# One PSUM tile for each unit's outputs, 64-row stores, and a last block emptied by VectorE and stored on two queues

## The chip, the cores and the metric

The kernel runs on one core of one Trainium2 chip. The metric is the device time of one execution in microseconds, less is better. A result is the median of several executions; all of those told here were fast ones. Every result was correct against the reference.

Engine names in the profile: PE is TensorE (PEld its weight loads), DVE is VectorE, ACT is ScalarE, POOL is GpSimd, SP is SyncE; a q behind the name is the engine's sequencer, which also issues DMAs.

## The reference, cut to what matters

An RWKV-5 attention (batch 4, 8 heads, 768 steps, head size 48) is followed by a dense block on 3072 rows of 384:

```python
x = attn_out.transpose(0, 2, 1, 3).reshape(3072, 384)
h = x @ w_in                 # 384 x 2048
g = h - np.tanh(h)
out = g @ w_out              # 2048 x 384
```

This text is about the last product and how its results leave the chip.

## The kernel before

The kernel works in 24 *units* of 128 rows, two units to a *block* (12 blocks). Every unit holds 64 steps of two batches, so its 128 output rows are two runs of 64 rows in memory. The dense part of a block goes in *tiles* of two slices of 128 of the 2048 columns: h (12 TensorE records), then five ScalarE and four VectorE steps that make g, then o (8 records). In the trace one fp32 matmul of the program shows as two records (768 records of o for 384 matmuls).

The first six blocks are done in four passes, a quarter of the columns each, because the weights are still being converted; their partial sums are kept in SBUF and VectorE adds each pass (`part`). So outputs are emptied 60 times from PSUM: 12 times by ScalarE and 36 times by VectorE in the passes, 12 times by ScalarE for the last six blocks.

```python
def o(self, t, half):
    if t.first and half == 0:
        pair = self.ps_d.tile([128, L, 512], F32, name="o", tag="o", bufs=1)   # both units
        self.outs = [pair[:, i, : self.d.DM] for i in range(L)]
    # the last tile finishes unit 0 (half 0) before unit 1 (half 1)
    for z, i in [(0, half), (1, half)] if t.last else [(half, 0), (half, 1)]:
        self.nc.tensor.matmul(self.outs[i], t.g2[:, z, i * C : (i + 1) * C], ...)

def empty(self, t, i):
    ...                                                  # VectorE adds in passes 2 to 4
    self.nc.scalar.copy(t.o, self.outs[i])

def store(self, t, i, queue):
    runs = self.rows(L * t.j + i)                        # two runs of 64 rows
    n, step = C // len(runs), runs[-1] - runs[0] or C
    to = bass.AP(tensor=self.out.tensor, offset=...,
                 ap=[[step * self.d.DM, len(runs)], [self.d.DM, n], [1, self.d.DM]])
    queue.dma_start(out=to, in_=t.o)                     # GpSimd; SyncE in the last block
```

`pair` holds 512 fp32 columns of PSUM for each unit. The framework that places the waits treats it as one tile: a write to it waits for earlier reads of it, whichever unit they were for.

In which order the instructions stand on each engine is decided on the host while the program is built. A small planner plays the list of tasks through with assumed costs and improves the order in 600 random tries with a fixed seed (`Random(3)`). The planner knows nothing of PSUM tiles. A change in the list of tasks therefore gives another order everywhere; a change in how a task is carried out does not.

At the end, every engine loads a flag and branches: a general path follows that is not taken here.

## Time and profile before

| of the kernel before | |
|---|---|
| time, median | 641.43 us (4 runs, 640.81 to 641.90) |
| span in the profile | 638.85 us |
| TensorE busy | 600.5 us, 94% |
| VectorE, ScalarE busy | 67%, 63% |
| last matmul ends | 625.18 us, 13.67 us before the end |

TensorE is the bound, so I read everything by what stops TensorE and by what follows its last matmul. The lines themselves are in the prediction. Two lines of the list of DMA issues are worth adding (out<-in, engine, count, size, median us from issue to landing): the stores of 192 KB on GpSimd's queue took over 7 us, while loads of half the size landed in 3.

```profile
rt<-in_r_dram SPq DMA_DIRECT2D x48, 96.0 KB, 3.1
...
out_dram<-part POOLq DMA_DIRECT2D x12, 192.0 KB, 7.5
out_dram<-o POOLq DMA_DIRECT2D x10, 192.0 KB, 7.7
```

### The profile page before, as it was taken

What the parts mean: (1) busy time and instruction counts of PE and PEld (TensorE: products, weight loads), DVE (VectorE), ACT (ScalarE), POOL (GpSimd) and SP (SyncE); (2) the same over time, 40 slices, a digit from 0 to 9 for tenths busy, and PEclk for the clock granted to TensorE, in tenths of its full rate; (3) what the DMA queues carried; (4) which work ended last, traced back from release to release, by engine and by line L of the source; (5) the groups of instructions that cost most, each with busy time, mean ns of one, the idle gap of its engine ahead of it and who ended that gap; (6) DMA issues with size and microseconds to landing.
All of it is one profiled execution on the core that took longest, in us unless ns stands there. A gap on an engine that the chain in (4) does not pass through costs nothing.

```text
span 638.9 us, 13183 instructions
## 1 busy us (share of the span) xinstructions
PE 600.5 (94%) x5297; PEld 442.1 (69%) x5297; DVE 430.1 (67%) x698; ACT 401.0 (63%) x875; POOL 56.1 (9%) x115
## 2 busy tenths in 40 slices
PE   8779999999999999999999999999999999999991
PEld 7657776676666666766777767777777777777760
DVE  5799887989895878665767665566755564645550
ACT  3487778868645656455764765666774667565550
POOL 3001111200000000001022011002010001011000
PEclk9999999999999999999999999999999999999996
DMA  7974796623310000001331220112210100000000
GB/s 128 177 163 94 133 189 119 131 59 103 99 50 0 1 1 1 1 2 38 68 75 35 58 44 8 44 33 39 51 32 1 33 8 9 24 7 8 20 0 30
DMA packets 92498, 33.76 MB, mean 53 GB/s; under 512 B 84900, under 2 KB 86384, under 8 KB 92428
## 3 DMA queue, kind: packets, MB, share of 16 engines
q1 hardware_dynamic: 82208, 27.34, 21.9%
q0 software_dynamic: 10208, 5.49, 3.6%
q8 instruction: 43, 0.70, 0.5%
q14 instruction: 27, 0.22, 0.1%
q10 hardware_dynamic: 12, 0.00, 0.0%
HBM read 26.94 MB, written 4.72 MB: 50 GB/s over the span
## 4 chain that ended last, share of the span: by engine, by line
PE 77%; DVE 10%; ACT 7%; issue 3%; DMA 1%; POOL 0%; DVEq 0%; ACTq 0%; POOLq 0%
PE o L202 33%; PE h L164 33%; PE yk_ps L564 5%; PE x_ps L606 3%; PE x_ps L564 1%; ACT tg L177 1%; DVE g L188 1%; DVE tg L190 1%; ACT s L173 1%; PE h L505 1%; ACT th L175 1%; DVE part L210 1%; DVE tg L192 1%; DVE g L194 1%; DVE rT L610 1%
## 5 line engine op out<-in xcount | busy, mean ns | idle before, releaser
L202 PE MATMUL o<-w_out_sb,g 128*128 128x384 f32 x768 | 283.3, 493 | 9.9 <-DVE part L210 8.5
L164 PE MATMUL h<-xt,w_in_sb 128*128 128x256 f32 x1152 | 281.3, 381 | 2.0 <-DVE w_in_sb L139 2.0
L164 PEld LDWEIGHTS h<-xt,w_in_sb 128*128 128x128 f32 x1152 | 216.2, 190 | 64.3 <-issue 2.2
L202 PEld LDWEIGHTS o<-w_out_sb,g 128*128 128x128 f32 x768 | 141.8, 191 | 79.3 <-DVE part L210 14.6
L188 DVE TENSOR_TENSOR g<-h,th 128x512 f32<-128x512 f32 x96 | 66.0, 687 | 78.6 <-ACT s L173 59.1
L177 ACT ACTIVATE tg<-h 128x512 f32<-128x512 f32 x96 | 57.0, 594 | 77.2 <-PE h L164 77.1
L190 DVE SCALAR_TENSOR_TENSOR tg<-s,tg 128x512 f32<-128x512 f32 x96 | 65.9, 686 | 47.6 <-ACT tg L177 25.1
L173 ACT ACTIVATE s<-h 128x512 f32<-128x512 f32 x96 | 57.3, 597 | 48.7 <-PE h L164 48.6
L175 ACT ACTIVATE th<-h 128x512 f32<-128x512 f32 x96 | 57.2, 595 | 31.1 <-PE h L164 30.9
L194 DVE COPY_PREDICATED g<-small,tg 128x512 f32<-128x512 int32 x96 | 70.4, 733 | 6.0 <-DVE tg L192 0.5
L192 DVE SCALAR_TENSOR_TENSOR tg<-q,tg 128x512 f32<-128x512 f32 x96 | 66.0, 688 | 7.5 <-ACT q L179 3.6
L179 ACT ACTIVATE q<-s,m1b 128x512 f32<-128x512 f32 x96 | 69.6, 725 | 0.7
L181 ACT ACTIVATE small<-s,smallb 128x512 f32<-128x512 f32 x96 | 69.4, 723 | 0.3
L706 POOL DMA_DIRECT2D xt<-rest x66 | 32.9, 505 | 223.8 <-ACT rest L692 223.8
L630 ACT ACTIVATE at<-same,du 128x64 f32<-128x64 f32 x160 | 41.8, 342 | 3.1 <-DVE du L626 2.8
L223 POOL DMA_DIRECT2D out_dram<-part x12 | 9.7, 808 | 218.6 <-DVE part L210 218.6
L610 DVE TENSOR_TENSOR rT<-x_ps,w_up 128x512 f32<-128x512 f32 x23 | 15.8, 686 | 12.7 <-PE x_ps L606 9.9
L210 DVE TENSOR_TENSOR part<-o,part 128x384 f32<-128x384 f32 x36 | 19.9, 552 | 6.0 <-PE o L202 6.0
L564 PEld LDWEIGHTS yk_ps<-at,vt 64*64 64x64 f32 x752 | 13.2, 134 | 12.7 <-DVE at L741 5.2
L564 PEld LDWEIGHTS yk_ps<-rT,state 48*64 48x64 f32 x704 | 12.3, 134 | 12.2 <-DVE state L712 5.6
L618 ACT COPY kT<-x_ps 128x512 f32<-128x512 f32 x22 | 12.9, 588 | 12.3 <-PE x_ps L606 7.6
L690 ACT COPY xt<-yk_ps 128x192 f32<-128x192 f32 x22 | 7.0, 320 | 21.1 <-PE yk_ps L564 20.9
(104 smaller groups left out, 427.5 us busy)
## 6 DMA issues: line engine op xcount, KB each, us to landing
st<-in_moe_w_out_dram SPq DMA_DIRECT2D x8, 768.0 KB, 7.0
rt<-in_r_dram SPq DMA_DIRECT2D x48, 96.0 KB, 3.1
vt<-in_v_dram SPq DMA_DIRECT2D x48, 96.0 KB, 3.2
st<-in_moe_w_in_dram SPq DMA_DIRECT2D x16, 288.0 KB, 5.5
kt<-in_k_dram SPq DMA_DIRECT2D x44, 96.0 KB, 3.5
out_dram<-part POOLq DMA_DIRECT2D x12, 192.0 KB, 7.5
out_dram<-o POOLq DMA_DIRECT2D x10, 192.0 KB, 7.7
st<-in_moe_w_in_dram SPq DMA_DIRECT2D x16, 96.0 KB, 5.4
```

The source lines that it names most:

```text
L164: self.nc.tensor.matmul(t.h2[:, z], self.w_in_sb[:, t.f // 2, kk, z * 128 : (z + 1) * 128], self.xts[t.j][:, kk].rearrange("p b t -> p (b ...
L173: A.activation(out, t.h, AF.Square)
L175: A.activation(out, t.h, AF.Tanh)
L177: A.activation(out, t.h, AF.Tanh, scale=G1)
L179: A.activation(out, t.s, AF.Square, bias=self.m1b)
L181: A.activation(out, t.s, AF.Relu, bias=self.smallb, scale=-1.0)
L188: V.tensor_tensor(t.g, t.h, t.th, ALU.subtract)
L190: V.scalar_tensor_tensor(t.tg, t.s, C4, t.tg, ALU.mult, ALU.mult)
L192: V.scalar_tensor_tensor(t.tg, t.q, K1, t.tg, ALU.add, ALU.mult)
L194: V.copy_predicated(t.g, t.small.bitcast(I32), t.tg)
L202: self.nc.tensor.matmul(self.outs[i], t.g2[:, z, i * C : (i + 1) * C], self.w_out_sb[:, t.f + z, :], start=t.first and z == 0, stop=t.last ...
L564: T.matmul(*args, skip_group_check=True, **how)
```

## The change

Its intent: unit 0 may be emptied while unit 1 is still being written; a store may use more of the DMA engines; and the last block, after which nothing else comes, may leave by the shortest way.

```diff
     def o(self, t, half):
         if t.first and half == 0:
-            pair = self.ps_d.tile([128, L, 512], F32, name="o", tag="o", bufs=1)
-            self.outs = [pair[:, i, : self.d.DM] for i in range(L)]
+            self.outs = [self.ps_o().tile([128, 512], F32, name=f"o{i}", tag=f"o{i}", bufs=1)[:, : self.d.DM]
+                         for i in range(L)]
...
-        self.nc.scalar.copy(t.o, self.outs[i])
+        if t.j == self.d.NB - 1:
+            self.nc.vector.tensor_copy(t.o, self.outs[i])
+        else:
+            self.nc.scalar.copy(t.o, self.outs[i])
-    def store(self, t, i, queue):
...            (one transfer of two runs)
+    def store(self, o, n, z, queue):
+        runs = self.rows(n)
+        size = C // len(runs)
+        queue.dma_start(out=self.out[runs[z] : runs[z] + size, :], in_=o[z * size : (z + 1) * size])
...
-                by = "SP" if j == d.NB - 1 else "POOL"
-                stored[j, i] = [add(by, .6, send, [x.empty[-1]], due + 4 * pace, data=.8)]
+                by = ["SP", "ACT"] if j == d.NB - 1 else ["POOL"] * 2
+                stored[j, i] = [add(by[z], .6, ..., [x.empty[-1]], due + 4 * pace, data=.4) for z in range(2)]
```

(Cut: a tile of 2 x 512 columns serves the first attention units before, from a pool of its own that is closed at the first output. The planner's task for the last emptying moves to VectorE. One `pace` is rewritten to the same value, and a call in the path that is not taken changes its arguments.) Since the tasks change, the search finds another order.

More of the change, by code (lines that the diff above doesn't have):

```diff
@@ L142, with __init__ @@
 class Dense:
-    def __init__(self, nc, work, gpool, ps_d, shared, out, rows):
-        self.nc, self.work, self.gpool, self.ps_d = nc, work, gpool, ps_d
+    def __init__(self, nc, work, gpool, ps_d, shared, out, rows, ps_o=None):
+        self.nc, self.work, self.gpool, self.ps_d, self.ps_o = nc, work, gpool, ps_d, ps_o or (lambda: ps_d)
         self.out, self.rows, self.xts, self.sums = out, rows, {}, {}
@@ L215, in empty @@
             t.o = self.sums[at] = self.work.tile([128, self.d.DM], F32, name="part", tag="part", bufs=L * FIRST)
-        self.nc.scalar.copy(t.o, self.outs[i])
-    def store(self, t, i, queue):
-        runs = self.rows(L * t.j + i)
-        n, step = C // len(runs), runs[-1] - runs[0] or C
-        to = bass.AP(tensor=self.out.tensor, offset=self.out[runs[0] :, :].offset,
-                     ap=[[step * self.d.DM, len(runs)], [self.d.DM, n], [1, self.d.DM]])
-        queue.dma_start(out=to, in_=t.o)
+        if t.j == self.d.NB - 1:
[6 more added lines that the diff above has]
+        queue.dma_start(out=self.out[runs[z] : runs[z] + size, :], in_=o[z * size : (z + 1) * size])
 ACT_STEPS, VEC_STEPS = ("s", "th", "tg", "q", "small"), ("g", "c1", "c2", "cp")
@@ L434, in near @@
     dense = Dense(nc, work, gpool, ps_d, shared, out,
-                  lambda n: [(n % 2 * 2 + z) * d.S + n // 2 * SHORT for z in range(2)])
+                  lambda n: [(n % 2 * 2 + z) * d.S + n // 2 * SHORT for z in range(2)], lambda: later())
     HALF = [slice(z * SHORT, (z + 1) * SHORT) for z in range(2)]
@@ L473, in near, with later @@
     ps, yk_ps = (ps_a.tile([128, 2, 512], F32, name=x, tag=x) for x in ("x_ps", "yk_ps"))
-    x_banks = [ps, ps_d.tile([128, 2, 512], F32, name="o", tag="o", bufs=1)]
+    early = ExitStack()
+    x_banks = [ps, early.enter_context(tc.tile_pool(name="n_ps_x", bufs=1, space=PSUM)).tile(
+        [128, 2, 512], F32, name="x2_ps", tag="x2_ps")]
+    pools = []
+    def later():
+        if not pools:
+            early.close()
+            pools.append(ctx.enter_context(tc.tile_pool(name="n_ps_o", bufs=1, space=PSUM)))
+        return pools[0]
     y_ps = yk_ps[:, :, :256].rearrange("e z (p t) -> e z p t", p=NP)
@@ L792, in run @@
                 ends.o = t.o
-            x.empty.append(add("DVE" if fs[0] else "ACT", .47, run, [[now, x.o][i]] + stored.get((j - 1, i), []), due + 3 * pace))
+            x.empty.append(add("DVE" if fs[0] or j == d.NB - 1 else "ACT", .47, run, [[now, x.o][i]] + stored.get((j - 1, i), []), due + 3 * pace))
             if whole:
-                def send(i=i, ends=ends):
-                    t.o = ends.o
-                    dense.store(t, i, e_of[by])
-                by = "SP" if j == d.NB - 1 else "POOL"
-                stored[j, i] = [add(by, .6, send, [x.empty[-1]], due + 4 * pace, data=.8)]
+                by = ["SP", "ACT"] if j == d.NB - 1 else ["POOL"] * 2
+                stored[j, i] = [add(by[z], .6, lambda z=z, i=i, ends=ends: dense.store(ends.o, L * j + i, z, e_of[by[z]]),
+                                    [x.empty[-1]], due + 4 * pace, data=.4) for z in range(2)]
     for n in range(L * (FIRST + 2)):
@@ L808, in near @@
             for f in range(done, done + part, 2):
-                pace = 5.2 + (3.7 if not done and j < FIRST - 1 else 1.25)
+                pace = 5.2 + (14.8 / part if not done and j < FIRST - 1 else 1.25)
                 hidden(j, (done, done + part), f, now, pace)
@@ L1029, in last @@
             second.empty(t, i)
-            second.store(t, i, nc.sync)
+            second.store(t.o, L * t.j + i, 0, nc.sync)
     def dense(j):
```

## The prediction

> **What bounds the kernel now.** I read the page first, then the stages, then the waits of TensorE, then single instructions, then the last 14 us. From the page of the kernel before:
>
> ```profile
> PE 600.5 (94%) x5297; PEld 442.1 (69%) x5297; DVE 430.1 (67%) x698; ACT 401.0 (63%) x875; POOL 56.1 (9%) x115
> ...
> PE 77%; DVE 10%; ACT 7%; issue 3%; DMA 1%; POOL 0%; DVEq 0%; ACTq 0%; POOLq 0%
> ...
> L202 PE MATMUL o<-w_out_sb,g 128*128 128x384 f32 x768 | 283.3, 493 | 9.9 <-DVE part L210 8.5
> ```
>
> TensorE is busy for 94% of the span and is most of the chain that ended last, so only what stops TensorE, or what comes after its last matmul, can be won. The third line names one thing that stops it: the output matmuls wait 8.5 us for the VectorE instruction that empties their PSUM tile. The busy times by stretch of the span (us, busy PE, PEld, DVE, ACT, POOL, clock, DMA share, GB/s) say where:
>
> ```profile
> 120.00:180.00 60.00, 57.33 (x218) 40.74 (x219) 53.77 (x84) 45.18 (x84) 0.00 (x0) 1.00 0.37 87
> 180.00:240.00 60.00, 56.83 (x217) 40.20 (x215) 45.07 (x73) 34.37 (x59) 0.00 (x0) 1.00 0.03 11
> 240.00:300.00 60.00, 57.16 (x277) 40.73 (x276) 40.45 (x63) 32.27 (x56) 2.98 (x4) 1.00 0.04 8
> ...
> 480.00:600.00 120.00, 119.78 (x890) 88.55 (x891) 64.85 (x100) 73.71 (x154) 10.82 (x18) 1.00 0.06 15
> 600.00:639.00 39.00, 24.44 (x89) 16.45 (x87) 11.78 (x18) 12.25 (x22) 0.00 (x0) 0.87 0.04 12
> ```
>
> From 120 to 300 us TensorE loses about 3 us in 60; from 480 to 600 nothing; after 600 there are 14 us with nothing to multiply. In the first of these stretches VectorE is at 53.77 of 60 (90%), later at 67 to 75%.
>
> One of the waits in the order of time (start, length, engine, line, operation):
>
> ```profile
> 158.18 1.45 PE L202 MATMUL o<-w_out_sb,g 128*128 128x384 f32 x4
> ...
> 159.47 1.46 PE L164 MATMUL h<-xt,w_in_sb 128*128 128x256 f32 x6
> ...
> 161.19 0.55 DVE L210 TENSOR_TENSOR part<-o,part 128x384 f32<-128x384 f32 x1
> ...
> 161.80 1.56 PE L202 MATMUL o<-w_out_sb,g 128*128 128x384 f32 x4 [0.87 <-DVE part L210]
> ...
> 163.39 0.56 DVE L210 TENSOR_TENSOR part<-o,part 128x384 f32<-128x384 f32 x1 [0.21 <-PE o L202]
> ```
>
> The four records at 158.18 finish unit 0 of a block, the emptying at 161.19 reads unit 0, the records at 161.80 finish unit 1, the emptying at 163.39 reads unit 1. The matmuls of unit 1 do not need unit 0 emptied: they wait only because both units lie in one tile, and a write to it waits for the earlier read. It is a false wait. The built program agrees: there the unit-1 matmuls wait for exactly that VectorE instruction.
>
> [...]
>
> [...] The store of before has an outer dimension of 2 on the memory side (two runs of 64 rows)[...]. The trace agrees in the last 12 us, where nothing else moves:
>
> ```profile
> 625.22 0.86 ACT L216 COPY o<-o 128x384 f32<-128x384 f32 x2 [4.52 <-PE o L202]
> 625.72 1.26 SPq L223 DMA_DIRECT2D out_dram<-o  x2
> ```
> ```profile
> 627.00:629.00 2.00, 0.00 (x0) 0.00 (x0) 0.00 (x0) 0.00 (x0) 0.00 (x0) 0.91 0.15 37
> 629.00:631.00 2.00, 0.00 (x0) 0.00 (x0) 0.00 (x0) 0.00 (x0) 0.00 (x0) 0.50 0.15 46
> ...
> 635.00:637.00 2.00, 0.00 (x0) 0.00 (x0) 0.00 (x0) 0.00 (x0) 0.00 (x0) 0.50 0.08 30
> ```
>
> A share of 0.13 to 0.15 is 2 of 16 engines, at some 50 GB/s. The packet records say the same: 256 packets of 1536 bytes, 65 ns each, from 626.96 to 636.63. 128 packets on each of two engines times 65 ns are 8.3 us.
>
> [...] So I give the second queue a few tenths, and the shape the rest.
>
> **The change part by part.**
>
> *Separate PSUM tiles.* A matmul record of the h group starts every 0.215 us and one of the o group every 0.3225 us when nothing stops them. I took each output matmul that began later than that. Nine times the last matmuls of unit 1 waited for the emptying of unit 0: 0.18, 1.03, 1.04, 0.43, 1.04, 0.87, 1.04, 0.55, 1.04, together 7.2 us. Five times the first matmul of the next block waited: 0.64, 0.38, 1.32, 1.32, 0.43, together 4.1 us. That is 11.3 us, more than the 8.5 + 0.5 us of idle time in the waits, because a stopped pipeline also loses its overlap. The first group vanishes whole, as nothing connects the two tiles. In the second group, three of the five (0.64 and the two of 1.32) had both emptyings back to back after the end of unit 1, since by then the emptying of unit 0 also waited for unit 1. In the built new program every emptying of unit 0 waits only for its own last matmul, and the next block's second matmul, not its first, waits for unit 1. That matmul comes 0.65 us (two records) later, behind some 1.3 us of h matmuls, against 0.55 us for an emptying. So these go too.
>
> Of the 11.3 us, 3.55 lie before 190 us, where VectorE is at 90% with the weight conversions: if TensorE is not stopped by this, it may be stopped by the next VectorE result. I count 60% there: 2.1 us. The other 7.75 lie where VectorE has a quarter or more free: I count all of it and 0.3 us for the slower first records after each stop. Sum 10.2 us.
>
> *64-row stores in the tail.* The end of before: last matmul 625.18, copies to 626.08, issues to 626.99, packets to 636.63, SyncE's wait for the second store over at 636.96, end at 638.85. [...] a store has 4 packets for each engine, 0.26 us by 65 ns each. The last transfer would be issued at about 625.75; its first packet comes 1.24 us after the issue (626.96 less 625.72), and the wait ends 0.33 us after the last packet: landed at 627.6. It stops being the bound. What then bounds is SyncE's own path: its issue ends at about 626.3, then it loads the flag that chooses the general path (2.46 us in before with the slow store behind it, 0.47 and 0.54 us on ScalarE and VectorE), then the branch (2.50 us to its next instruction), then some 8 waits of 0.065 us, then 1.69 us from the last such wait to the end. That makes 631.7 to 633.7, against 638.85: 5.2 to 7.2 us won, 6.2 in the middle. The second queue is worth at most the second issue of 0.56 us on SyncE, and is in this sum.
>
> *VectorE empties the last block.* A VectorE read of 128x384 from PSUM takes 0.55 us with an add; ScalarE's copy took 0.48. Nothing is won in that alone. But unit 0 is now emptied at about 623.9 instead of 625.22, so its stores leave before unit 1 ends and only unit 1 remains on the path. It is in the sum above.
>
> *Elsewhere.* GpSimd issues 44 smaller stores in place of 22 (two per unit; it is busy 9% and took 0.8 us for an issue): some 18 us more of its time, on no path. Work on TensorE is unchanged except for three fewer filling matmuls at the start.
>
> Sum: 641.87 - 10.2 - 6.2 = 625.5. The kernel's order comes out of a randomised search, and the changed dependencies move it: the first loads, the converted pieces and the attention steps stand in another order. TensorE idles 11.6 us before 60 us, so I allow 2 us either way there and put 0.5 us against me: 626.0.
>
> **The rivals.**
>
> *VectorE takes over as the bound up to 190 us.* For it: 53.77 of 60 busy. Against: those waits are only 3.5 us. Then the gain there is zero, and 628 results.
>
> *The wait only moves to the next block's unit 1.* The new order often puts the two emptyings back to back, so the second stands late. For it: five waits of before were of that kind. Against: about 1.9 us of matmuls lie between. If half of the 11.3 us stayed, 631.
>
> *The tail is hidden by the exit anyway.* For it: flag load and branch need 5 us after the last issue; that is in my sum. If the flag load took another 2.5 us on both queues, or ScalarE's issues and exit came later than SyncE's, the tail would give 4 us: 628.
>
> *The new order of the start is worse by several us.* For it: nothing in the profile tells; TensorE's waits on VectorE there (2.0, 2.0, 1.0 us) depend on who comes first. It could as well be better.
>
> **Range and chances.** Everything right with a lucky order gives 622; two rivals together give 631. Faster by over 2% means under 629.0. I give that 0.82, within 2% 0.17, slower 0.01.
>
> **What would show it.** In the changed profile: TensorE's waits for the emptying instruction under 1.5 us in all; 180 to 300 us with TensorE at over 59 of 60; in the last slice a short burst on many DMA engines instead of 0.13 for 10 us; under 9 us from the last matmul to the end. Wrong would be: waits of the output matmuls on VectorE's g, or of the h matmuls on ScalarE, in place of the old ones; VectorE near 58 of 60 before 190 us; or a last matmul as late as before, relative to a start that has grown.

## The result, and the profile after

The changed kernel takes 623.34 us in the median (4 runs, 622.38 to 624.55), the kernel before 641.43. The ratio is 0.9719 with a 95% interval of 0.9695 to 0.9744. Ratios here are the mean time of one kernel's fast runs over the mean of the other's in the same rounds, so they are not quite the ratio of the medians quoted. The profiled execution is one of the two slower ones of the four (624.55 us at a mean granted TensorE clock of 0.989; the two at 622.38 us had 0.995). Its trace has three stretches of 3.4 us at half clock between 36 and 57 us, where the kernel before has one.

The page after, the lines that answer to those of before:

```profile
PE 599.2 (96%) x5291; PEld 444.7 (71%) x5291; DVE 429.5 (69%) x700; ACT 399.6 (64%) x873; POOL 60.5 (10%) x137
...
PE 82%; DVE 4%; issue 4%; DMA 3%; ACT 3%; SPq 1%; POOL 1%; DVEq 0%; ACTq 0%; POOLq 0%
...
L202 PE MATMUL o<-w_out_sb,g 128*128 128x384 f32 x768 | 279.5, 489 | 1.9 <-DVE g L194 1.9
```

The work is the same (599.2 us against 600.5). The idle time in front of the output matmuls fell from 9.9 to 1.9 us, and what is left waits for g, not for an emptying. The stretches of the span show it by stage (the columns are those of the prediction):

```profile
120.00:180.00 60.00, 60.00 (x237) 43.80 (x236) 52.38 (x85) 45.55 (x90) 0.00 (x0) 1.00 0.32 67
180.00:240.00 60.00, 60.00 (x234) 44.08 (x233) 49.59 (x79) 36.82 (x63) 0.00 (x0) 1.00 0.20 46
240.00:300.00 60.00, 60.00 (x351) 43.90 (x350) 42.67 (x68) 37.65 (x73) 5.21 (x10) 1.00 0.11 24
...
480.00:600.00 120.00, 119.01 (x827) 87.25 (x826) 64.59 (x100) 72.64 (x153) 11.02 (x22) 1.00 0.06 13
```

From 120 to 300 us TensorE is never idle; before it lost 8.7 us there. VectorE is not saturated: 52.38 of 60 us. The place in the order of time that answers to the one in the prediction:

```profile
159.50 1.45 PE L202 MATMUL o<-w_out_sb,g 128*128 128x384 f32 x4
...
161.15 0.55 DVE L210 TENSOR_TENSOR part<-o,part 128x384 f32<-128x384 f32 x1
...
162.09 1.45 PE L202 MATMUL o<-w_out_sb,g 128*128 128x384 f32 x4
...
163.70 0.54 DVE L210 TENSOR_TENSOR part<-o,part 128x384 f32<-128x384 f32 x1
```

Unit 1's four records start 2.59 us after unit 0's, which is just four records of o and six of h; before it was 3.62 us. The tail, first in the order of time, then by stretches:

```profile
613.61 0.56 DVE L217 COPY o<-o 128x384 f32<-128x384 f32 x1 [1.65 <-PE o L202]
614.20 1.80 SPq L225 DMA_DIRECT2D out_dram<-o  x2
614.20 1.78 ACTq L225 DMA_DIRECT2D out_dram<-o  x2
614.90 0.56 DVE L217 COPY o<-o 128x384 f32<-128x384 f32 x1 [0.73 <-PE o L202]
```
```profile
615.00:617.00 2.00, 0.00 (x0) 0.00 (x0) 0.46 (x1) 0.00 (x0) 0.00 (x0) 1.00 0.52 131
617.00:619.00 2.00, 0.00 (x0) 0.00 (x0) 0.00 (x0) 0.00 (x0) 0.00 (x0) 1.00 0.30 86
619.00:621.00 2.00, 0.00 (x0) 0.00 (x0) 0.00 (x0) 0.00 (x0) 0.00 (x0) 0.74 0.01 4
```

Unit 0 is emptied at 613.61, before the last matmul ends at 614.86. The DMA share is 0.52 where it was 0.15, and the last packet of the stores ends at 617.79 instead of 10 us after the issue. The packet records also show 4-byte packets beside the stores: 2 for each store before (with its 128 packets of 1536 bytes), 16 for each 64-row store now (with its 64). That fits 2 and 16 engines, as does the number of 1536-byte packets in flight at once (2 during 7.6 of 9.7 us before, 14 to 17 during 1.1 of 2.4 us now). VectorE's copy of unit 0 runs from 613.61 to 614.17, while TensorE still writes unit 1's columns (its last record ends at 614.86), and the results are correct: the prediction took this for granted, and here it is shown. The end comes 7.97 us after the last matmul (13.67 before). So of the 16.0 us between the two spans, 10.3 lie before the last matmul and 5.7 behind it. The stores on GpSimd's queue, on no path, show the same effect: 2.1 us to landing where they took 7.7.

```profile
out_dram<-part POOLq DMA_DIRECT2D x24, 96.0 KB, 2.2
out_dram<-o POOLq DMA_DIRECT2D x20, 96.0 KB, 2.1
```

This agrees with the prediction. But it does not tell which part of the change did it: the order of instructions is another one too.

### The profile page after: what moved, and what is told of

The parts are those of the page before. It is cut to its first block, busy times and chain, and to the rows that moved or that the text cites. A ratio compares the mean times of both kernels' runs of the same rounds, so it can differ in the third digit from the quotient of the medians.

```text
span 622.8 us, 13185 instructions
## 1 busy us (share of the span) xinstructions
PE 599.2 (96%) x5291; PEld 444.7 (71%) x5291; DVE 429.5 (69%) x700; ACT 399.6 (64%) x873; POOL 60.5 (10%) x137
## 4 chain that ended last, share of the span: by engine, by line
PE 82%; DVE 4%; issue 4%; DMA 3%; ACT 3%; SPq 1%; POOL 1%; DVEq 0%; ACTq 0%; POOLq 0%
PE h L164 37%; PE o L202 37%; PE yk_ps L575 4%; PE x_ps L617 2%; PE x_ps L575 1%; SPq L605 1%; DMA vt<-in_v_dram 1%; POOL xt L717 1%; DMA xt<-rest 1%; DMA first_k<-in_k_dram 1%; DVE at L752 1%; DVE rT L621 1%; DMA st<-in_moe_w_in_dram 0%; ACT at L641 0%; ACT kT L629 0%
## 5 line engine op out<-in xcount | busy, mean ns | idle before, releaser
L202 PE MATMUL o<-w_out_sb,g 128*128 128x384 f32 x768 | 279.5, 489 | 1.9 <-DVE g L194 1.9
L225 POOL DMA_DIRECT2D out_dram<-part x24 | 12.5, 525 | 202.5 <-DVE part L210 202.3
L629 ACT COPY kT<-x_ps 128x512 f32<-128x512 f32 x22 | 12.9, 588 | 18.9 <-PE x_ps L617 13.8
L752 DVE COPY_PREDICATED at<-before,x_ps 128x512 f32<-128x512 int32 x24 | 17.4, 726 | 10.3 <-PE x_ps L575 10.3
L575 PE MATMUL yk_ps<-at,vt 64*64 64x64 f32 x752 | 16.9, 228 | 5.0 <-DVE at L752 3.1
```

Source lines behind the costliest of these rows:

```text
L575: T.matmul(*args, skip_group_check=True, **how)
```

## The experiments

My theory: the shared tile's false waits and the shape of the stores make up nearly all of the gain. The rivals: the new order makes the gain; the second queue makes the gain in the tail; VectorE's emptying matters. Twelve kernels ran, in three groups of four; each group was timed against the kernel before on its own chip, five rounds each. "Lost to emptyings" is read from the trace as in the prediction: how much later than the usual 0.215 or 0.3225 us after its predecessor a matmul record began when an emptying released it.

| kernel | order | PSUM tiles | stores | median us | before there | ratio | lost to emptyings us | tail us |
|---|---|---|---|---|---|---|---|---|
| before | old | shared | 2 runs | 641.43 | | | 11.3 | 13.7 |
| e1_tiles | old | separate | 2 runs | 630.19 | 642.30 | 0.9810 | 0 | 12.9 |
| e2_shape | old | shared | 64 rows | 637.48 | 642.30 | 0.9920 | 11.3 | 9.8 |
| e3_queues | old | shared | 2 runs, 2 queues | 643.25 | 642.30 | 1.0019 | 11.3 | 13.9 |
| e4_tiles_shape | old | separate | 64 rows | 625.40 | 642.30 | 0.9731 | 0 | 7.8 |
| after | new | separate | 64 rows, 2 queues | 623.34 | 641.43 | 0.9719 | 0 | 8.0 |
| a1_one_queue | new | separate | 64 rows, 1 queue | 623.13 | 642.64 | 0.9705 | 0 | 7.6 |
| a2_scalar_empties | new | separate | as after | 623.65 | 642.64 | 0.9700 | 0 | 7.8 |
| a3_pair_tile | new | shared | as after | 626.62 | 642.64 | 0.9760 | 1.7 | 7.7 |
| a4_seed4 | new, seed 4 | separate | as after | 620.60 | 642.64 | 0.9654 | 0 | 8.1 |
| a5_pair_seed4 | new, seed 4 | shared | as after | 626.82 | 642.69 | 0.9760 | 3.4 | 8.1 |
| a4_seed5 | new, seed 5 | separate | as after | 621.68 | 642.69 | 0.9669 | 0 | 8.2 |
| b4_seed4 | old tasks, seed 4 | shared | 2 runs | 635.66 | 642.69 | 0.9897 | 4.4 | 13.9 |
| b4_seed5 | old tasks, seed 5 | shared | 2 runs | 638.27 | 642.69 | 0.9935 | 6.9 | 13.8 |

The interval of a ratio is about 0.0015 to 0.0033 to each side, that is 1 to 2 us.

### One part alone, in the old order

**e1_tiles** takes only the PSUM part of the diff. The instructions of TensorE, VectorE and ScalarE stand in the order of before, one for one.

```diff
-            pair = self.ps_d.tile([128, L, 512], F32, name="o", tag="o", bufs=1)
-            self.outs = [pair[:, i, : self.d.DM] for i in range(L)]
+            self.outs = [self.ps_o().tile([128, 512], F32, name=f"o{i}", tag=f"o{i}", bufs=1)[:, : self.d.DM] ...]
```

> The kernel before with the two units' outputs in separate PSUM tiles and nothing else; every engine's order of instructions stays that of before. Theory (false waits): TensorE loses none of the 11.3 us at these waits from 120 to 350 us, the last matmul ends at about 613 to 614 us instead of 625.2, and in the last block the emptying of unit 0 starts before unit 1's matmuls end; the tail keeps its 10 us of store. Time 629 to 631. Rival (the new order of the search did it): the time stays within 2 us of before, 640 or more. Rival (VectorE takes over before 190 us): 632 to 634, with new waits of the output matmuls on VectorE's g.

630.19 us: the theory's number. The waits for an emptying are gone. The stretch from 120 us, and TensorE's waits after 60 us, show what took their place:

```profile
120.00:180.00 60.00, 59.33 (x229) 42.32 (x229) 56.14 (x88) 45.65 (x86) 0.00 (x0) 1.00 0.43 100
```
```profile
PE o L202 <- DVE g L194: 1.6, 4, 0.7
```

VectorE rises to 56.14 of 60 us, and before 190 us four matmuls that had no wait for g now have one: they start 0.45, 0.23, 0.25 and 0.40 us late, 1.3 us together (the kernel before had one such wait there, of 0.27 us, which is gone). The line just shown counts only idle times long enough for the view: those at 120.71, 179.21, 447.57 (also new, 0.53 us late) and 612.02 (which before has too). So the rival with VectorE is real, and small.

**e2_shape** cuts each store in two, on the queues of before.

```diff
-        queue.dma_start(out=to, in_=t.o)                        # [[2 runs], [64 rows], [384]]
+        for z, at in enumerate(runs):
+            queue.dma_start(out=self.out[at : at + n, :], in_=t.o[z * n : (z + 1) * n])
```

> The kernel before with each store cut into two 64-row transfers on the same queue as before, same order. Theory (shape decides the number of DMA engines): the last stores are over about 2 to 3 us after their issue, the DMA share in the tail rises from 0.14 to 0.3 or more, and the end comes 5 to 6 us sooner: 635.5 to 637. Rival (only the second queue helps): within 1 us of before. Nothing changes before the last block.

637.48 us, a ratio of 0.992, that is 5.1 us: the gain is at the low end of the 5 to 6 us expected, and the absolute time is 0.5 us above its range. The share in the tail rises as expected:

```profile
629.00:631.00 2.00, 0.00 (x0) 0.00 (x0) 0.00 (x0) 0.00 (x0) 0.00 (x0) 0.81 0.39 96
```

The tail is 9.77 us and not 8: with the shared tile both units are emptied only after the last matmul, so all four issues come late, one after the other on SyncE; the fourth alone takes 1.63 us, and the exit follows at 630.6.

**e3_queues** tests the second queue without the shape.

```diff
-                    dense.store(t, i, e_of[by])
+                    dense.store(t, i, A if by == "SP" and i == 1 else e_of[by])
```

> The kernel before with the last block's unit 1 stored from ScalarE's queue and unit 0 from SyncE's, each still one transfer of two runs of 64 rows. Theory: both use the same two DMA engines, 128 packets of 65 ns on each, so the data still ends some 10 us after the issue; the second issue comes 0.5 us sooner at most. Time within 1 us of before, 640.5 to 641.5. Rival (two queues are two paths): the data phase halves and the time falls by about 4 us, to 637.

643.25 us against 642.30: no gain at all (my absolute range was too low, because before itself ran at 642.3 on that chip). The stretches of the tail have the same share as in the kernel before, two engines of 16, although two queues are at work:

```profile
629.00:631.00 2.00, 0.00 (x0) 0.00 (x0) 0.00 (x0) 0.00 (x0) 0.00 (x0) 0.68 0.15 44
631.00:633.00 2.00, 0.00 (x0) 0.00 (x0) 0.00 (x0) 0.00 (x0) 0.00 (x0) 0.50 0.15 44
633.00:635.00 2.00, 0.00 (x0) 0.00 (x0) 0.00 (x0) 0.00 (x0) 0.00 (x0) 0.50 0.13 49
```

**e4_tiles_shape** joins the edits of e1 and e2.

> The kernel before with separate PSUM tiles and 64-row stores on the old queues, ScalarE emptying, order of before. Theory: the two gains add up, 11.5 and 5.5 us: 624 to 625.5, so that the order of the new search, the second queue and VectorE's emptying together are worth 1 us or less. Rival: the gains overlap or the rest matters, then 627 or more.

625.40 us, as expected. 0.9810 and 0.9920 lose 1.9% and 0.8%; together 0.9731 loses 2.7%. The two parts add up, and reach the changed kernel (0.9719) within their intervals. Had I stopped here, I would have written that the new order is worth nothing.

### One part undone, in the new order

**a1_one_queue** and **a2_scalar_empties** take back the small parts.

```diff
-  dense.store(ends.o, L * j + i, z, e_of[by[z]])
+  dense.store(ends.o, L * j + i, z, Q if j == d.NB - 1 else e_of[by[z]])      # a1
-        if t.j == self.d.NB - 1:
-            self.nc.vector.tensor_copy(t.o, self.outs[i])
-        else:
-            self.nc.scalar.copy(t.o, self.outs[i])
+        self.nc.scalar.copy(t.o, self.outs[i])                                # a2
```

> The changed kernel with all four last stores issued from SyncE, the rest as it is. Theory (the shape made the gain, the second queue only saves issue time): SyncE's last issue ends some 0.5 to 1.6 us later, the rest of its exit follows, 623.8 to 625. Rival (the second queue carries the tail): 626 or more.

> The changed kernel with ScalarE emptying the last block, as before, in the new order. Theory: the copy takes 0.48 us instead of 0.56 and nothing else depends on it; within 1 us of the changed kernel, 622.4 to 624.4. Rival (VectorE's emptying is worth something): 625 or more.

623.13 and 623.65 us: neither part is worth anything measurable (a1 came out 0.7 us below the range I gave, which had it slower than the changed kernel). With one queue SyncE's last issue ends later relative to the last matmul (1.8 against 1.1 us), as expected, but the branch at the exit then took 2.55 us against 3.43, so that a1's tail is even the shorter one, 7.6 against 8.0 us.

**a3_pair_tile** takes the separate tiles back and leaves everything else.

```diff
-            self.outs = [self.ps_o().tile([128, 512], F32, name=f"o{i}", tag=f"o{i}", bufs=1)[:, : self.d.DM] ...]
+            pair = self.ps_o().tile([128, L, 512], F32, name="o", tag="o", bufs=1)
+            self.outs = [pair[:, i, : self.d.DM] for i in range(L)]
```

> The changed kernel with both units in one PSUM tile again, everything else as it is, so the instructions stand in the new order. Theory: the false waits come back, TensorE's waits for the emptying go from 0 to some 8 us of idle time, 632 to 636. Rival (the new order carries the gain): under 627.

626.62 us. This expectation failed: taking the tiles apart is worth 12 us in the old order and only 3 to 4 us in the new one. The waits for an emptying, 8.5 us of idle time in the kernel before, in this kernel:

```profile
PE o L202 <- DVE part L210: 1.8, 3, 0.8
```

The false dependence is still there, in the built program unit 1's matmuls wait for the emptying of unit 0 in nearly every block (16 of the 18 places where VectorE empties). It bites less, because VectorE gets to the emptying sooner. This is the place shown above, in a3:

```profile
158.13 1.45 PE L202 MATMUL o<-w_out_sb,g 128*128 128x384 f32 x4
...
158.56 0.69 DVE L188 TENSOR_TENSOR g<-h,th 128x512 f32<-128x512 f32 x1 [2.66 <-ACT tg L177]
...
159.77 0.55 DVE L210 TENSOR_TENSOR part<-o,part 128x384 f32<-128x384 f32 x1
...
160.71 1.45 PE L202 MATMUL o<-w_out_sb,g 128*128 128x384 f32 x4
```

The steps before the emptying in VectorE's queue start at 158.56, 0.43 us after the four records of unit 0, so the emptying is over at 160.32 and unit 1 starts on time at 160.71. In the kernel before the first of them had to wait for ScalarE and started 1.81 us after unit 0's records. So a part of my theory falls. The waits were the cause, but the tile was only one of two things that made them; the order that the planner found was the other. The traces say where the emptyings stand: of the 18 emptyings of unit 0 on VectorE, 2 directly follow the last step of a tile (the one that makes g) in the kernel before, and 9 do so here. I tested the order only as a whole, not the place of a single emptying.

### Is it the order, and is it luck?

The new theory: with a shared tile the cost is decided by the order, anything from 2 to 11 us; with separate tiles the order does not matter. The rival: the new list of tasks gives better orders by itself. Four kernels with other seeds of the planner's search, the only edit in three of them:

```diff
-        chance = Random(3)
+        chance = Random(4)      # or Random(5)
```

> The changed kernel with another seed of the search (4 instead of 3): an order as good as any by the search's own lights. Theory (the order is luck of one or two us): within 2 us of the changed kernel, 621.5 to 625.5. Rival (the order of the changed kernel is a lucky one worth much of the gain): 627 or more.

> The changed kernel with a third seed, 5. Emptyings of unit 0 stand late in VectorE's queue in most places. Theory (with separate tiles their place does not matter): 620 to 625 and no wait of TensorE for an emptying. Rival (it still matters): 627 or more.

620.60 and 621.68 us, with no wait for an emptying in either. With separate tiles three orders out of three lose nothing there, and their times lie within 3 us. The order still matters for something else: on the same chip seed 4 (0.9654, interval 0.9640 to 0.9669) is clear of a1 and a2 (0.9705 and 0.9700, intervals from 0.9685 up), by some 3 us. Where they come from is not shown. Seed 4 was 0.9 us better than the range I gave; it is the fastest kernel of this study, 0.9654 of the time before.

> The kernel before with seed 4 instead of 3, shared tile and old stores. Of the 18 emptyings of unit 0 on VectorE some ten stand at once after the last step of a tile, against two in the kernel before. Theory: the false waits shrink to about half, 633 to 638. Rival (the order that the search finds for the old tasks always pays the 11 us): 640 or more.

> The kernel before with seed 5, shared tile and old stores. Some six of 18 emptyings stand at once after the last step. Theory: in between, 634 to 641. Rival (the order does not matter here): within 1 us of before.

635.66 and 638.27 us, both as expected, by the seed alone. TensorE's waits in the two, b4_seed4 first:

```profile
PE o L202 <- DVE part L210: 3.0, 5, 0.9
```
```profile
PE o L202 <- DVE part L210: 4.5, 13, 0.9
```

The kernel before lost 11.3 us to emptyings, these lose 4.4 and 6.9. The differences of 6.9 and 4.4 us answer to the differences in time, 7.0 and 4.4 us (642.69 less 635.66 and 638.27). That they agree to a tenth is luck: the intervals are 1.5 to 2 us wide to each side, and other waits differ too. So of three orders of the old tasks the kernel before had the worst, and seeds move the loss without any change of tasks. The rival is not excluded: with the shared tile the old tasks lose 11.3, 4.4 and 6.9 us, the new ones 1.7 and 3.4 (a3 above, a5 below). All new ones lie below all old ones, but five orders are too few to say that the new list gives better ones by itself.

**a5_pair_seed4** is a3 with seed 4.

> The changed kernel with another seed of the search and with both units in one PSUM tile again. With seed 3 the pair tile cost only 3.3 us, as many emptyings of unit 0 stand at once after VectorE's last step of a tile there. With seed 4 most stand behind steps of the next tile, as in the kernel before. Theory (what the shared tile costs is decided by where the emptying stands in VectorE's queue): 627 to 631, that is 6 to 10 us above the same order with separate tiles (620.6), with waits for the emptying of 4 us or more. Rival (the shared tile costs some 3 us in any new order): 623 to 625.

626.82 us, 6.2 us above the same order with separate tiles. That is the low end of the 6 to 10 us expected (the time is 0.2 us below its range), but not by the waits alone: it loses 3.4 us to emptyings, with the line below, where I had said 4 us of waits or more.

```profile
PE o L202 <- DVE part L210: 2.3, 6, 0.7
```

In the profiled runs the last matmul of the two kernels is 3.8 us apart (615.58 and 611.79), which fits the 3.4. The other 2 to 3 us of the medians stay unexplained; a5's runs spread from 624.4 to 630.5, and the two kernels were timed on different chips.

## Why the prediction was right or wrong

The predicted 626.0 us with 621.5 to 630.5 holds the measured 623.34, and "faster by over 2%" came true. By its steps:

**What bounds the kernel** was right: TensorE's stops and the tail. The two together give the whole difference of the spans.

**Separate tiles.** Right in the mechanism and near in size. I took 11.3 us of lost starts (2.3 more than the idle time of 9.0: a record of o lasts 0.49 us in the trace and the next one starts 0.32 us after it, and this overlap is lost at a stop), counted 10.2 of it, and the edit alone gave 12.1 us (642.30 to 630.19); 0.8 of that is in the tail, where unit 0's store leaves earlier. All 14 late matmuls are on time in e1, apart from those that now wait for g.

**60% before 190 us, because VectorE takes over.** In the old order this is what happened: of 3.55 us, 1.3 came back as waits for g, where before had 0.3, so some 70% were won. In the order that the changed kernel really has, no idle time is left from 120 to 300 us, so there it was all won.

**The tail.** Right: 5.7 us, predicted 5.2 to 7.2. SyncE's last issue ended 1.1 us after the last matmul, as worked out. The flag load took 1.06 us, inside the range. The branch took 3.43 us instead of 2.50, which is what is missing from the middle of the range. Data no longer bound it: the last packet ended 2.9 us after the last matmul. It ended 2.3 us after the start of its issue where the sum has 1.5 (1.24 and, by my estimate, four packets for each engine of 65 ns, the median of the two last stores before; the 64 packets of one store took 0.47 to 0.89 us in all), which cost nothing. The cause is the shape: e2 has it (a share of up to 0.39) and e3 does not (up to 0.15). The 3.43 us are not the branch instruction, which took 0.05. The trace has an 8 KB packet of the kind "instruction" in this gap: it starts 0.9 us after SyncE's branch both before and after (630.50 and 618.10), and SyncE's next instruction comes 1.6 us later before, 2.5 us later after. In the changed kernel two more such packets start at 617.79 and 617.88, and VectorE and ScalarE, which had branched at 615.69 and 616.85, go on at 620.41 and 620.46. What SyncE waits for in this gap, and why it is longer after, is not shown: no run tests it.

**The second queue and VectorE's emptying** were given a few tenths, which was my estimate; they are worth nothing measurable (ratios of 0.9705 in a1 and 0.9700 in a2, 0.9719 with both). One thing was missed: with a shared tile the second queue seems to help. a3's tail with two queues is 7.7 us, e2's with one is 9.8, although both empty the units only after the last matmul. No run has the queue as the only difference there, but the traces speak for it: the first issue starts 0.63 and 0.54 us after the last matmul, and SyncE's last one ends after 1.81 us with two issues (a3) and after 4.05 with four (e2).

**"I allow 2 us either way" for the new order.** This step failed as it was put. I looked for the effect of the order at the start of the kernel, where the trace shows nothing of the kind: TensorE's idle time before 60 us is 11.6 us in both profiles. The order acts in the middle. With the tile shared, the new order alone wins most of what the separate tiles win: a3 has a ratio of 0.976, and 6.0 of its 15.4 us lie in the tail by its profile (13.67 less 7.69), so some 9 us are the order's (an estimate from a ratio and a profile). The sum came out right because separate tiles and the new order remove the same waits. The 10 to 12 us must not be counted twice, and they cannot be given to one part: asked from the old order the tiles win 12 us, asked from the new one 3 to 4, from seed 4's 6.

**GpSimd's time**, on no path, was overestimated: 22 more stores of 0.8 us were to cost some 18 us. The smaller stores took 0.53 us each, and GpSimd's busy time rose from 56.1 to 60.5 us.

**The rivals.** "The wait only moves to the next block's unit 1" did not happen in any of the seven kernels with separate tiles: no record there waits for an emptying. "The tail is hidden by the exit anyway" is true in part: what bounds the tail now is the flag load and the gap after the branch, with 1.06 and 3.43 of its 8 us.

## What to carry to other kernels

Outputs that are emptied one after the other want a PSUM tile each: in this kernel's framework waits go by tile, and a shared tile makes the time depend on the order that a scheduler happens to find (1.7 to 11.3 us lost in five orders). When a change goes through a scheduler, test the parts from both ends, alone in the old order and undone in the new one, and run a second seed: each end by itself would have told a false story here. For a DMA, try another shape of the side in memory: here a store with an outer dimension of 2 there used 2 engines of 16, at a share of 0.13 to 0.15, and stores with 64 there, by the packet counts, all 16, at a share of 0.52 over 2 us in the changed kernel.
